# Attention with two gated layers: the stacking transfers in another order, and one turn on GpSimd alone

## The chip, the cores and the metric

The kernel runs on one core of one Trainium2 chip. The metric is the device time of one execution in microseconds (us). A core has the engines TensorE (PE in the profile, its weight loads PEld), VectorE (DVE), ScalarE (ACT), GpSimd (POOL) and SyncE (SP, which here issues every DMA transfer).

## The reference

Four batches, eight heads, 576 positions, 64 numbers per head. The reference rotates q and k by position, takes the softmax attention, and puts the result through two dense layers with gates and a normalisation. Cut to what matters here:

```
q_rot, k_rot = rotate(q), rotate(k)
scores = (1/8) * q_rot @ k_rot^T                       # per batch and head, 576 x 576
attn = exp(scores - rowmax) / (rowsum + 1e-9)
x = (attn @ v) as 2304 tokens x 512
x = (sigmoid(x @ w_gate) * (x @ w_val)) @ w_out         # d_ff 1536
h = x @ w_in; s = h * softmax(h); out = layernorm(s) * g_ln @ w_out2
```

## The kernel before

The work is in three stages. The attention stage goes over 16 **pairs** of heads, each pair in 9 tiles of query rows (four of 128 rows for each head, and in the middle one tile of the 64 left-over rows of both heads). The gate stage and the last stage follow.

fp32 operands are split into a high part (fp32r, made by ScalarE, the `CAST`s of L431) and a low part (the rest, made by VectorE, the `TENSOR_TENSOR`s of L434), so that a product is high x high + high x low + low x high. For the scores of head `h`, TensorE wants high and low parts of k or q on top of one another in the 128 partitions. The first tile of a pair (`st0`: blocks `flat[0]` to `flat[3]` = high k, high q, low k, low q, with head 0 in partitions 0 to 63 and head 1 in 64 to 127) is filled by the evacuations of three transpositions (`qk_bank`: `tq` on TensorE, L303 and L306). Then `stack` moves halves between partitions by DMA: the rows of head 1 go out of `st0` into the second tile `st1`, and when they have been read, the rows of head 0 are copied into the places they left. Those two last transfers (L318, L319 of the kernel before) overwrite what the first three read, so SyncE waits for these before it issues them. The first scores of a pair (L369, tile 0) read `st0` in full: the first product reads what L318 wrote, the second what L319 wrote. From there on TensorE goes on in order; a product that waits holds everything behind it.

Before the transpositions q and k are turned (`turn`: two products, L245, into `other` and in place, then a difference and a sum, L253, into `turned`). For pairs 2 to 15 GpSimd does that, while the pair before is computed. Pair 0 is turned at the start by VectorE and GpSimd together; pair 1 in the kernel before by GpSimd (head 0) and, after the first row maximum, by VectorE (head 1).

The order on each engine is written out by hand: an agenda of slots relative to the pair's first tile (`SLOTS`, L534 on), which the loop at L719 goes through tile by tile: row maximum (L376, VectorE), evacuations (ScalarE, then the exponentials, then VectorE), the next tile's scores on TensorE, then the rest of the slot, among it the DMA issues on SyncE. All instructions of an engine run in the order in which they were issued, and SyncE's too.

The sums of the exponentials (one column of `sum` for each tile) are inverted, transposed, written to a small DRAM buffer and spread over the partitions by DMA (`spread`, L416), by which GpSimd scales the attention's output (L426). GpSimd also makes the low part of v (L287), copies the left-over columns (L340) and adds the output's halves (L493).

Of the kernel before, what the change touches and what calls it, by code (L numbers as in the profile page):

```python
# [20 lines left out]
def kernel(  # L21
# [21 lines left out]
    nc = tc.nc  # L43
    B, H, S, D = q.shape
# [3 lines left out]
    P = 128  # L48
    MAIN, LEFT, HALF = 512, 64, 288
# [258 lines left out]
            src = ps[:, 0:P].rearrange("p (a t) -> p a t", a=2)  # L308
        return [(h_out, l_out, src)]

    def stack(i):
        s0, s1 = stacks[i, 0].bitcast(F32), stacks[i, 1].bitcast(F32)
        flat = s0.rearrange("p a b s -> p (a b) s")
        dma = nc.sync.dma_start
        dma(out=s1[D:P], in_=flat[D:P, 0:3])
        dma(out=s1[0:D, 0:2], in_=flat[D:P, 2:4])
        dma(out=s1[0:D, 2], in_=flat[D:P, 0])
        dma(out=flat[D:P, 0:2], in_=flat[0:D, 2:4])  # L318
        dma(out=flat[D:P, 2], in_=flat[0:D, 0])  # L319

    def stack_first(h, step):

# [23 lines left out]

    order = [(0, 0), (0, 1), (0, 2), (0, 3), None, (1, 0), (1, 1), (1, 2), (1, 3)]
    NTL = len(order)
    sum_at = [0, 1, 2, 3, 8, 4, 5, 6, 7]
    e_tiles = {}  # L350
    sums = {}
    wts = {}
# [26 lines left out]
    def exps(i, n, ps, nm):  # L379
        e = e_p.tile([P, S], F32, tag="e", name=f"e{i}_{n}")  # L380
        nc.scalar.activation(  # L381
            out=e.rearrange("p (j c) -> p j c", j=2),
            in_=ps[:, :, :HALF],
            func=AF.Exp,
            bias=nm,
            accum_out=sums[i][:, sum_at[n]:sum_at[n] + 1],
        )
        e_tiles[i, n] = e

# [21 lines left out]
    def spread(i):  # L411
        d = wts[i]
        w = wt_p.tile([P, S], F32, tag="wt", name=f"wt{i}")
        for c0, n, at in ((0, MAIN, 0), (MAIN, LEFT, 2 * MAIN)):
            for h in range(2):
                nc.sync.dma_start(  # L416
                    out=w[h * D:(h + 1) * D, c0:c0 + n],
                    in_=d[at + h * n:at + (h + 1) * n].unsqueeze(0).to_broadcast([D, n]),
                )
        wts[i] = w  # L420

    def scale_x(i):
# [107 lines left out]
    def at(g, kind, fn, *args):  # L530
        agenda.setdefault((g, kind), []).append((fn, args))
# [13 lines left out]
        scale=24,  # L545
        turn=(-16, -16, -15, -15),
        bank=(-11, -9, -8),
        stack=-6,
        split_v=-1,
        stack_left=0,  # L550
        load_qk=-23,
# [4 lines left out]
        sum_eng=0,  # L556
        uw=(1, 0, 0, 0),
        bank1=(1, 1, 1),
        stack1=3,
        first_b=(-1, -1, 2),  # L560
        turn1=(0, 0, 0, 0),
        split_v0=0,
        stack_left0=0,
    )
# [27 lines left out]
    for i in range(NPR):  # L592
        g = i * NTL
        own = SLOTS_FIRST if i == 0 else SLOTS_LAST if i == NPR - 1 else SLOTS
        for n in range(NTL):
            at(g + own["te"][n], FIRST, transpose_e, i, n)
        at(g + own["corner"], GROUP, transpose_corner, i)
        for h in range(2):
            at(g + own["left"][h], GROUP, transpose_left, i, h)
            for j in range(2):  # L600
                m0 = 0
                for slot, m1 in own["av"][2 * h + j]:
                    at(g + slot, ATTEND, attend, i, h, j, m0, m1)
                    m0 = m1
            at(g + own["join"][h], REST, join, i, h)
            at(g + own["add"][h], REST, add, i, h)
        for name, fn in (
            ("weigh", weigh), ("weigh_t", weigh_t), ("weigh_out", weigh_out), ("spread", spread), ("scale", scale_x)
        ):
            at(g + own[name], REST, fn, i)  # L610

        if i > 1:
            at(max(0, g + SLOTS["load_qk"]), REST, lambda i: [None for _ in load_qk(i)], i)
            at(max(0, g + SLOTS["load_v"]), REST, load_v, i)
            for m, slot in enumerate(SLOTS["turn"]):
                at(max(0, g + slot), REST, turn, i, m)
        if i > 0:
            for part, slot in enumerate(SLOTS["bank"] if i > 1 else [b - NTL for b in SLOTS["bank1"]]):
                at(g + slot, GROUP, qk_bank, i, part)
            at(g + (SLOTS["stack"] if i > 1 else SLOTS["stack1"] - NTL), REST, stack, i)  # L620
            at(g + SLOTS["split_v"], REST, split_v, i)
            at(g + SLOTS["stack_left"], REST, stack_left, i)
    cur, late, moved = [], [], []
# [62 lines left out]
    if True:  # L686

        spare_1 = et_p.tile([P, 16 * S], F32, tag="et", name="spare1")
        table = spare_1[:, 2 * NSL * D:2 * NSL * D + 2 * 5 * D // 2].rearrange("p (c i d) -> p c i d", c=2, i=5)
        first_loads = load_qk(0)  # L690
        next(first_loads)
        nc.sync.dma_start(out=table, in_=rope)
        for _ in first_loads:
            pass
        for h in range(2):
            nc.scalar.activation(out=rope_sb[:, :, h, 4:8], in_=table[:, :, 0:4], func=AF.Copy, scale=D ** -0.5)
        for _ in load_qk(1, spare_1[:, 0:2 * NSL * D].rearrange("p (h i d) -> p h i d", h=2, i=NSL)):
            pass
        nc.sync.dma_start(out=g_sb, in_=moe2_g_ln.rearrange("(k p) -> p k", p=P))
        load_v(0)  # L700
        load_v(1)
        turn_first(table)
        for h in range(2):
            nc.scalar.copy(out=rope_sb[:, :, h, 0:4], in_=table[:, :, 0:4])
            nc.scalar.copy(out=rope_sb[:, :, h, 8:9], in_=table[:, :, 4:5])
        first.extend(qk_bank(0, part)[0][2] for part in range(3))
        for m in range(3):
            stack_first(0, m)
            at(SLOTS["first_b"][m], REST, stack_first, 1, m)
        at(SLOTS["stack_left0"], REST, stack_left, 0)  # L710
        at(SLOTS["split_v0"], REST, split_v, 0)
        for m in range(4):
            turn(1, m, slice(0, 1))
            at(SLOTS["turn1"][m], REST, turn, 1, m, slice(1, 2), nc.vector)
        for fn, args in agenda.pop((-1, REST), []):
            fn(*args)

        sc = scores(0, 0)
        for g in range(NPR * NTL):  # L719
            i, n = divmod(g, NTL)  # L720
            if g == (NPR - 1) * NTL:
                prep_ctx.close()
                xs_pool["p"] = x_ctx.enter_context(tc.tile_pool(name="xs", bufs=XS, side="right", reuse_waits="tile"))
            if g == 1:
                et = et_p.tile([P, 2, 2, 4, S], F32R, tag="et", name="et")
            nm = row_max(i, n, sc)
            if SLOTS["exp_pos"] == 0:
                exps(i, n, sc, nm)
            evacuate_h(cur)
            if SLOTS["exp_pos"] == 1:  # L730
                exps(i, n, sc, nm)
            evacuate_h(late)
            if SLOTS["exp_pos"] == 2:
                exps(i, n, sc, nm)
            evacuate_u()
            if SLOTS["exp_pos"] == 3:
                exps(i, n, sc, nm)
            evacuate_l()
            if g + 1 < NPR * NTL:
                sc = scores(*divmod(g + 1, NTL))  # L740
            advance(g)
# [381 lines left out]
```

## Time and profile before

| what | value |
|---|---|
| time, median of 3 runs | 967.11 us (964.16 to 969.16) |
| the profiled execution's own time | 964.83 us |
| its span, first to last instruction | 963.1 us |
| busy over the span: PE, DVE, ACT, POOL | 96%, 67%, 52%, 46% |
| attention stage, roughly | 0 to 310 us |
| gate stage, roughly | 310 to 740 us |
| last stage | 740 to 963 us |

The page of the profile lists busy time by engine, forty slices of the span, the DMA queues, the chain of work that ended last (followed back from the last instruction to what released each one), groups of instructions by line with the idle time before them and who ended it, and the DMA issues with the time from issue to landing. In the slices of the attention stage, PE, DVE and ACT are each busy for eight or nine tenths and more, and POOL for seven to nine; in the other stages PE alone is full. Names such as `s`, `te`, `av`, `tq`, `st` are the kernel's tiles without their numbers, so `st` stands for `st0` and `st1` alike.

### The profile page before, as it was taken

The numbers are of one execution on the slowest core, as the hardware profiler recorded it, in microseconds if no ns is written. First come the engines' busy times: TensorE is split into PE (matmuls) and PEld (weight loads), VectorE is DVE, ScalarE is ACT, GpSimd is POOL, SyncE is SP. The second block draws the span as 40 slices with busy tenths as digits, with TensorE's granted clock in tenths as the row PEclk, the third lists the DMA queues.
The fourth block names the chain that finished last, engine by engine and source line by source line (L and its number), as shares of the span: only waits on it lengthen the run. The fifth ranks groups of instructions, "written<-read, shape, count | busy, mean of one in ns | idle before, by whom it ended". The sixth has DMA issues, their size and how long they took to land.

```text
span 963.1 us, 14429 instructions
## 1 busy us (share of the span) xinstructions
PE 923.1 (96%) x5128; PEld 801.5 (83%) x5128; DVE 647.7 (67%) x1073; ACT 501.7 (52%) x994; POOL 444.0 (46%) x356
## 2 busy tenths in 40 slices
PE   4999999899999899999999999999999989999998
PEld 3889889899898688898788898788898768888886
DVE  7999989999888955346345355545456787666661
ACT  4888989898987323133111123112123576666662
POOL 5668879889845533344324344324343531111110
PEclk9999999999999999999999999999999999999999
DMA  3666677676754310103101012100112334334332
GB/s 108 141 169 165 152 191 180 160 188 159 160 141 122 104 66 22 44 23 94 38 22 44 23 45 88 44 22 22 44 46 71 103 64 90 66 72 93 66 77 44
DMA packets 92311, 86.10 MB, mean 89 GB/s; under 512 B 52608, under 2 KB 77456, under 8 KB 92240
## 3 DMA queue, kind: packets, MB, share of 16 engines
q1 hardware_dynamic: 92240, 85.19, 35.7%
q8 instruction: 40, 0.66, 0.3%
q14 instruction: 31, 0.25, 0.1%
HBM read 46.83 MB, written 4.79 MB: 54 GB/s over the span
## 4 chain that ended last, share of the span: by engine, by line
PE 63%; DVE 14%; DMA 10%; POOL 4%; issue 4%; ACT 2%; SPq 2%; DVEq 0%; POOLq 0%; ACTq 0%
DMA st<-st 9%; PE gv L680 9%; PE gv L681 9%; PE gv L679 9%; PE y L790 4%; PE y L789 4%; PE y L788 4%; PE po L977 3%; PE po L976 3%; PE po L978 3%; PE ph L881 3%; PE ph L882 3%; PE ph L883 3%; DVE nm L376 3%; DVE et L434 2%
## 5 line engine op out<-in xcount | busy, mean ns | idle before, releaser
L774 POOL TENSOR_TENSOR gs<-g,gs 128x512 fp32r<-128x512 f32 (+1 forms) x59 | 74.1, 1257 | 261.2 <-DVE gs L773 203.9
L769 ACT ACTIVATE sg<-gv 128x512 f32<-128x512 f32 (+1 forms) x60 | 33.3, 555 | 288.2 <-PE gv L681 288.2
L679 PE MATMUL gv<-xs,w 128*128 128x512 f32 (+1 forms) x480 | 177.4, 370 | 2.1 <-ACT w L137 2.1
L681 PE MATMUL gv<-xs,w 128*128 128x512 f32 (+1 forms) x480 | 177.5, 370 | 1.2 <-POOL w L138 1.2
L680 PE MATMUL gv<-xs,w 128*128 128x512 f32 (+1 forms) x480 | 177.4, 370 | 1.0 <-DVE xs L514 1.0
L771 DVE TENSOR_TENSOR g<-gv,sg 128x512 f32<-128x512 f32 (+1 forms) x60 | 38.2, 636 | 174.5 <-ACT sg L769 164.9
L381 ACT ACTIVATE e<-s,nm 128x576 f32<-128x576 f32 x144 | 107.3, 745 | 16.9 <-DVE nm L376 16.4
L369 PE MATMUL s<-st 128*128 128x288 f32 x512 | 102.8, 319 | 13.8 <-DMA st<-st 7.0
L376 DVE TENSOR_REDUCE nm<-s 128x1 f32<-128x576 f32 x144 | 107.2, 745 | 5.5 <-PE s L369 4.0
L681 PEld LDWEIGHTS gv<-xs,w 128*128 128x128 f32 x480 | 90.9, 189 | 17.3 <-POOL w L138 2.1
L680 PEld LDWEIGHTS gv<-xs,w 128*128 128x128 f32 x480 | 90.5, 189 | 17.5 <-DVE xs L514 2.7
L679 PEld LDWEIGHTS gv<-xs,w 128*128 128x128 f32 x480 | 90.5, 188 | 17.4 <-ACT w L137 2.5
L434 DVE TENSOR_TENSOR et<-te,et 128x512 fp32r<-128x512 f32 x144 | 98.3, 684 | 9.7 <-ACT et L431 8.5
L481 PE MATMUL av<-et,vs 128*128 128x288 f32 x512 | 99.9, 316 | 0.3 <-DVE uw L632 0.3
L369 PEld LDWEIGHTS s<-st 128*128 128x128 f32 x512 | 75.3, 193 | 23.2 <-DMA st<-st 6.3
L790 PE MATMUL y<-gs,w 128*128 128x512 f32 (+1 forms) x240 | 88.3, 368 | 0.0
L789 PE MATMUL y<-gs,w 128*128 128x512 f32 (+1 forms) x240 | 88.2, 368 | 0.0
L788 PE MATMUL y<-gs,w 128*128 128x512 f32 (+1 forms) x240 | 88.2, 367 | 0.0
L440 PE MATMUL te<-ident,e 128*128 128x128 f32 x576 | 87.0, 274 | 0.7 <-DVE et L434 0.7
L431 ACT CAST et<-te 128x512 fp32r<-128x512 f32 x144 | 84.2, 586 | 5.3 <-PE te L440 5.2
L481 PEld LDWEIGHTS av<-et,vs 128*128 128x128 f32 x512 | 73.0, 189 | 1.6 <-DVE uw L632 1.0
L440 PEld LDWEIGHTS te<-ident,e 128*128 128x128 f32 x576 | 71.1, 141 | 1.1 <-DVE et L434 0.9
(128 smaller groups left out, 1958.1 us busy)
## 6 DMA issues: line engine op xcount, KB each, us to landing
wraw<-in_moe_w_out_dram SPq DMA_DIRECT2D x20, 512.0 KB, 4.6
st<-st SPq DMA_DIRECT2D x30, 288.0 KB, 3.1
st<-st SPq DMA_DIRECT2D x15, 432.0 KB, 4.0
wraw<-in_moe_w_gate_dram SPq DMA_DIRECT2D x12, 512.0 KB, 4.0
wraw<-in_moe_w_val_dram SPq DMA_DIRECT2D x12, 512.0 KB, 4.5
um<-uw SPq DMA_DIRECT2D x32, 144.0 KB, 2.4
st<-st SPq DMA_DIRECT2D x30, 144.0 KB, 4.9
rawv<-in_v_dram SPq DMA_DIRECT2D x16, 256.0 KB
```

Of the source, the lines that this page charges most:

```text
L369: nc.tensor.matmul(ps[:, j, :HALF], w, x, start=m == 0, stop=m == len(mm) - 1)
L376: nc.vector.tensor_reduce(out=nm, in_=ps[:, :, :HALF], axis=AX.XY, op=ALU.max, negate=True)
L381: nc.scalar.activation(out=e.rearrange("p (j c) -> p j c", j=2), in_=ps[:, :, :HALF], func=AF.Exp, bias=nm, accum_out=sums[i][:, sum_at[n] ...
L434: nc.vector.tensor_sub(out=l_out, in0=ps, in1=h_out.bitcast(F32))
L440: nc.tensor.transpose(ps[:, r * P:(r + 1) * P], e[:, r * P:(r + 1) * P], ident)
L481: nc.tensor.matmul(av[:, :HALF], *mm[m], start=m == 0, stop=m == len(mm) - 1)
L679: nc.tensor.matmul(ps[:, :n], wh, x[:, 0, :n], start=kk == 0, stop=False)
L680: nc.tensor.matmul(ps[:, :n], wh, x[:, 1, :n], start=False, stop=False)
L681: nc.tensor.matmul(ps[:, :n], wl, x[:, 0, :n], start=False, stop=kk == KD - 1)
L788: nc.tensor.matmul(ys[m][:, :n], wh, g[:, 0, :n], start=first, stop=False)
L789: nc.tensor.matmul(ys[m][:, :n], wl, g[:, 0, :n], start=False, stop=False)
L790: nc.tensor.matmul(ys[m][:, :n], wh, g[:, 1, :n], start=False, stop=last)
```

## The change

Three things change.

1. `stack` issues six transfers in place of five, in another order. The bytes are the same. The first two read only high parts, which ScalarE makes; the low parts, which VectorE makes, come with the third and the fourth. The transfer of 432 KB (three blocks) is divided into 288 KB and 144 KB, and the smaller one goes to the fourth place.
2. The columns of `sum` stand in the order of the tiles, so the left-over row comes in the middle, and `spread` needs three transfers in place of four.
3. GpSimd turns both heads of pair 1, with instructions twice as wide; VectorE's four instructions for head 1 go away.

```
     def stack(i, step):
         ...
-        dma(out=s1[D:P], in_=flat[D:P, 0:3])
-        dma(out=s1[0:D, 0:2], in_=flat[D:P, 2:4])
-        dma(out=s1[0:D, 2], in_=flat[D:P, 0])
-        dma(out=flat[D:P, 0:2], in_=flat[0:D, 2:4])
-        dma(out=flat[D:P, 2], in_=flat[0:D, 0])
+        if step == 0:
+            dma(out=s1[D:P, 0:2], in_=flat[D:P, 0:2])
+            dma(out=s1[0:D, 2], in_=flat[D:P, 0])
+            dma(out=s1[0:D, 0:2], in_=flat[D:P, 2:4])
+            dma(out=s1[D:P, 2], in_=flat[D:P, 2])
+        else:
+            dma(out=flat[D:P, 0:2], in_=flat[0:D, 2:4])
+            dma(out=flat[D:P, 2], in_=flat[0:D, 0])
...
-            accum_out=sums[i][:, sum_at[n]:sum_at[n] + 1],
+            accum_out=sums[i][:, n:n + 1],
...
-        for c0, n, at in ((0, MAIN, 0), (MAIN, LEFT, 2 * MAIN)):
-            for h in range(2):
-                nc.sync.dma_start(
-                    out=w[h * D:(h + 1) * D, c0:c0 + n],
-                    in_=d[at + h * n:at + (h + 1) * n].unsqueeze(0).to_broadcast([D, n]),
-                )
+        for h, c0, n, at in ((0, 0, S, 0), (1, 0, MAIN, S + LEFT), (1, MAIN, LEFT, S)):
+            nc.sync.dma_start(
+                out=w[h * D:(h + 1) * D, c0:c0 + n], in_=d[at:at + n].unsqueeze(0).to_broadcast([D, n])
+            )
...
-        stack=-6,
+        stack=(-6, -6),
...
-        stack1=3,
+        stack1=(3, 3),
...
         for m in range(4):
-            turn(1, m, slice(0, 1))
-            at(SLOTS["turn1"][m], REST, turn, 1, m, slice(1, 2), nc.vector)
+            turn(1, m)
```

Both steps of `stack` stand in the same slot, where the five transfers stood. The first place is SyncE's queue around the stacking of pair 3 (`st_3_679` or `st_3_676` is `st0`, `st_3_680` or `st_3_677` is `st1`; a name behind "waits" is what the instruction waits for, where DMAHW0 to DMAHW7 are eight counters of landed transfers). Before:

```order
L315 DMA st_3_680<-st_3_679 64x1728 [waits DMAHW3_49,DVE_49]
L316 DMA st_3_680<-st_3_679 64x1152 [waits DMAHW4_49]
L317 DMA st_3_680<-st_3_679 64x576 [waits DMAHW5_49]
L318 DMA st_3_679<-st_3_679 64x1152 [waits DMAHW6_49,DMAHW5_49,DMAHW3_49]
L319 DMA st_3_679<-st_3_679 64x576 [waits DMAHW7_49,DMAHW4_49]
```

And of the change:

```order
L317 DMA st_3_677<-st_3_676 64x1152 [waits Activation_49]
L318 DMA st_3_677<-st_3_676 64x576 [waits DMAHW5_49]
L319 DMA st_3_677<-st_3_676 64x1152 [waits DMAHW6_49,DVE_49]
L320 DMA st_3_677<-st_3_676 64x576 [waits DMAHW7_49]
L322 DMA st_3_676<-st_3_676 64x1152 [waits DMAHW5_49,DMAHW4_49,DMAHW0_49]
L323 DMA st_3_676<-st_3_676 64x576 [waits DMAHW7_49,DMAHW6_49,DMAHW1_49]
```

The first transfer now waits for ScalarE in place of VectorE, and the first of the two overwriting transfers now waits for the first and second reading transfer (counters 4 and 5; before: for the first and the third, counters 3 and 5), the second one for the third and fourth.

The second place is GpSimd's queue at the start, from the turn of pair 1 to that of pair 2, as a difference:

```order
-L245 TENSOR_TENSOR other_206<-spare_134,rope_sb 128x576 [waits DMAHW5_49,DMAHW0_49,DMAHW6_49,DVE_49,DMAHW7_49,Activation_49,Pool_49]
-L245 TENSOR_TENSOR spare_134<-spare_134,rope_sb 128x576 [waits Pool_49]
-L253 TENSOR_TENSOR turned_209<-spare_134,other_206 128x9x32 [waits PE_49,Pool_49]
-L253 TENSOR_TENSOR turned_209<-spare_134,other_206 128x9x32
...
+L245 TENSOR_TENSOR other_206<-spare_134,rope_sb 128x1152 [waits DMAHW5_49,DMAHW0_49,DMAHW6_49,DVE_49,DMAHW7_49,Activation_49,Pool_49]
+L245 TENSOR_TENSOR spare_134<-spare_134,rope_sb 128x1152 [waits Pool_49]
+L253 TENSOR_TENSOR turned_209<-spare_134,other_206 128x2x9x32 [waits PE_49,Pool_49]
+L253 TENSOR_TENSOR turned_209<-spare_134,other_206 128x2x9x32
```

The four instructions stay in their place and are twice as wide; on VectorE the four of head 1 (two of L245, two of L253) that stood between the first and the second row maximum are gone.

## Rows read from the trace of the kernel before

**Rows 1.** Busy time by stretch: stretch, length, then each engine's busy us (instructions), clock.
```profile
50.60:68.19 17.59, 16.81 (x131) 16.11 (x132) 16.17 (x28) 15.84 (x38) 13.19 (x10) 1.00 0.65 156
...
sum 246.74, PE 235.41 PEld 224.81 DVE 228.20 ACT 221.08 POOL 198.46; mean PE 16.81 PEld 16.06 DVE 16.30 ACT 15.79 POOL 14.18
...
330.00:740.00 410.00, 408.57 (x2004) 345.14 (x2003) 203.93 (x310) 95.30 (x175) 152.02 (x118) 1.00 0.14 46
```

**Rows 2.** Waits, 33 to 282 us: who for whom, total us, times, longest.
```profile
POOL vs L287 <- ACT vs L286: 32.0, 12, 7.6
...
PE s L369 <- DMA st<-st: 7.0, 16, 1.1
...
DVE uw L632 <- PE av L481: 5.4, 11, 0.6
```

**Rows 3.** SyncE's issues in order of time, stacking of pair 2: start, us, what.
```profile
40.40 0.54 SPq L315 DMA_DIRECT2D st<-st  x1
41.00 0.59 SPq L316 DMA_DIRECT2D st<-st  x1
41.64 1.67 SPq L317 DMA_DIRECT2D st<-st  x1
46.70 0.46 SPq L318 DMA_DIRECT2D st<-st  x1
47.26 0.54 SPq L319 DMA_DIRECT2D st<-st  x1
```

**Rows 4.** DMA issues of the page: times, KB each, median us from issue to landing.
```profile
st<-st SPq DMA_DIRECT2D x15, 432.0 KB, 4.0
um<-uw SPq DMA_DIRECT2D x32, 144.0 KB, 2.4
```

**Rows 5.** The chain of waits, 38 to 71 us: start, us, what.
```profile
41.64 5.01 DMA st<-st
...
47.26 3.30 DMA st<-st
...
50.60 0.67 PE s L369 x3
...
57.22 0.28 DVE st L434
```

**Rows 6.** The start in order of time, 10 to 29 us: start, us, engine, what.
```profile
10.18 1.40 POOL L245 TENSOR_TENSOR other<-spare,rope_sb 128x576 f32<-128x576 f32 x1 [1.51 <-DVE turned L253]
...
11.66 1.40 POOL L245 TENSOR_TENSOR spare<-spare,rope_sb 128x576 f32<-128x576 f32 x1
11.88 1.50 DVE L334 CAST st<-st 64x576 fp32r<-64x576 f32 x1
...
14.73 0.62 POOL L340 CAST qtl<-st 128x64 fp32r<-128x64 f32 x2
...
15.81 0.76 DVE L245 TENSOR_TENSOR other<-spare,rope_sb 128x576 f32<-128x576 f32 x1
...
17.34 1.57 POOL L287 TENSOR_TENSOR vs<-rawv,vs 128x640 fp32r<-128x640 f32 x1 [1.98 <-ACT vs L286]
17.39 2.20 DVE L253 TENSOR_TENSOR turned<-spare,other 128x288 f32<-128x288 f32 x2
...
19.73 2.64 POOL L245 TENSOR_TENSOR other<-raw,rope_sb 128x1152 f32<-128x1152 f32 x1 [0.82 <-DVE turned L253]
19.74 1.94 PE L303 MATMUL tq<-ident,turned 128*128 128x128 f32 x8 [1.72 <-DVE turned L253]
...
22.45 2.63 POOL L245 TENSOR_TENSOR raw<-raw,rope_sb 128x1152 f32<-128x1152 f32 x1
...
23.26 2.14 DVE L334 CAST st<-st 64x576 fp32r<-64x576 f32 x1
...
25.16 2.88 POOL L253 TENSOR_TENSOR turned<-raw,other 128x576 f32<-128x576 f32 x2
25.43 0.76 DVE L376 TENSOR_REDUCE nm<-s 128x1 f32<-128x576 f32 x1
```

More of the change, by code (lines that the diff above doesn't have):

```diff
@@ L309, in qk_bank, with stack @@
         return [(h_out, l_out, src)]
-    def stack(i):
+    def stack(i, step):
         s0, s1 = stacks[i, 0].bitcast(F32), stacks[i, 1].bitcast(F32)
@@ L348 @@
     NTL = len(order)
-    sum_at = [0, 1, 2, 3, 8, 4, 5, 6, 7]
     e_tiles = {}
@@ L558 @@
         bank1=(1, 1, 1),
-        stack1=3,
+        stack1=(3, 3),
         first_b=(-1, -1, 2),
-        turn1=(0, 0, 0, 0),
         split_v0=0,
@@ L619 @@
                 at(g + slot, GROUP, qk_bank, i, part)
-            at(g + (SLOTS["stack"] if i > 1 else SLOTS["stack1"] - NTL), REST, stack, i)
+            for step, slot in enumerate(SLOTS["stack"] if i > 1 else [s - NTL for s in SLOTS["stack1"]]):
+                at(g + slot, REST, stack, i, step)
             at(g + SLOTS["split_v"], REST, split_v, i)
```

## The prediction

> **What bounds the kernel now.** I read the busy time by stretch first. In the gate stage TensorE is busy for 408.57 of 410 us [rows 1], and the change doesn't touch it. The attention stage is another matter: over 14 pairs, 246.74 us, TensorE is busy for 235.41 and VectorE for 228.20, that is 16.81 and 16.30 us in a pair of 17.62 on average [rows 1]. So about 0.8 us of each pair is lost on the fullest engine, 11.3 us in all. Second, the waits in that stretch: 7.0 us of those 11.3 are TensorE's score products waiting for the stacking transfers, 16 times, at most 1.1 us [rows 2]. Third, SyncE's issues and the chain of waits, which show why these transfers are late. In pair 2 the first stacking transfer is issued at 40.40, the third lands at 41.64 + 5.01 = 46.65; only then is the first overwriting transfer issued (46.70), and the second one (47.26) lands 3.30 later, at 50.56. The score product starts at 50.60 [rows 3, 5]. From the first issue to the last landing that is 10.16 us. From the product at 50.60 the chain comes to the last evacuation of the next pair's transposes at 57.50 [rows 5], some 7 us, and there the next stacking starts. 10.2 + 7, and what lies between, is the pair's 17.59 us [rows 1]. The stage runs in a loop through the stacking, and TensorE's own 16.8 us are the next bound, close behind.
>
> **The stacking transfers.** Same bytes, one issue more, another order. The first three transfers of before, 432 + 288 + 144 = 864 KB, have all landed 6.25 us after the first issue (46.65 - 40.40), and the first 432 KB alone take 4.0 [rows 3, 4]. So data flows without a gap at 432 KB in 2.25 us, or 0.75 for 144 KB, and only the first transfer shows a fixed part, of about 1.75. Of the new order the first two are again 432 KB: landed at 4.0 to 4.1. The first overwriting transfer waits for these two alone and is issued at 4.1 in place of 6.3. Its 288 KB come behind the third and fourth transfer, which land at 6.25 as the same 864 KB did: 6.25 + 1.5 = 7.75. The second one is issued at 6.3. It then takes between 2.4 (a transfer of the same size alone, tile um [rows 4]) and 3.30 (the same transfer behind another's data [rows 5]), so it lands 8.7 to 9.6 after the first issue in place of 10.16. I take 8.9, since it is issued 2.2 us behind the other and that one is nearly through: 1.2 us earlier, the bounds 0.5 and 1.5. That covers the longest wait for one transfer, 1.1 us. So by the rows a transfer that queues behind others adds no fixed part: the second and third of before added 432 KB in 2.25 us [rows 3, 4]. The Trainium skill (DMA: Bandwidth & Descriptors, Anatomy of one DMA) says otherwise for a single one, some 2.0 us of fixed cost whatever its size, mostly for the receipt of the last byte, measured on transfers that GpSimd issues; if each of the six added its own, the sum would be a loss, by an estimate from the page 14 times 2.0 = 28 us. By the rows it is the gain worked out next, and the fourth rival is what is left of the doubt.
>
> The extra issue costs SyncE 0.5 to 0.6 us [rows 3] in a time in which it otherwise stands waiting for the landing; if that cover were gone, the loads behind it would be 0.6 later. The long issue of 1.67 [rows 3] comes with the transfer that goes past 720 KB; it will now be the fourth, which ends at about 3.4, still before 4.0. That the first two wait for ScalarE and not for VectorE gives up to 0.6 us more where SyncE is free, and nothing where it is busy issuing; I count nothing.
>
> What is it worth? At most the 7.0 us [rows 2]. At least nothing, if TensorE's lost time is only moved to a wait for VectorE or ScalarE, which are nearly as full. VectorE itself waits 5.4 us for TensorE in the same stretch [rows 2], behind such stalls, so they are not free. With the loop through the stacking open, a pair is held by TensorE's 16.8 and VectorE's 16.3 us; I take seven tenths: **4.9 us**.
>
> GpSimd, whose turns feed the next pair, is not in the way: at its low part of v it still waits for ScalarE, 32.0 us in 12 times [rows 2], and pairs shorter by 0.35 us take little of that.
>
> **The turn of pair 1.** VectorE loses four instructions between its first and second row maximum, from 15.81 to 19.59 [rows 6], 3.8 us in which nothing else of it runs; TensorE's transposes started behind them at 19.74. Now they wait for GpSimd. It starts at 10.18 as before, and its four instructions of full width take what they take for pair 2, from 19.73 to 28.04, 8.3 us [rows 6]: done at 18.5, with 0.25 us more if VectorE's copy gets between them. The transposes start 0.15 later, at 18.65 to 18.9: 0.8 to 1.1 us earlier. Next comes VectorE's copy at L334. It took 2.14 us at 23.26 and 1.50 at 11.88, and both times ended 0.32 after an instruction of GpSimd that was running (25.08 and 13.06) [rows 6]: it stands still while GpSimd's instruction lasts. The first copy is now held by an instruction that ends at 12.82, 0.2 us earlier than before. For the second: GpSimd is done with the turn at 18.5 to 18.75, its copies and low part of v (0.62 and 1.57 [rows 6]) take it to about 20.9, and its next instruction runs until about 23.6. The copy comes to its place at about 22.3 and ends 0.32 after that, at 23.9, where it ended at 25.40. So the row maximum that started at 25.43 is 1.5 us earlier. I take **1.3 us** for the start, between the 0.8 of the transposes and 1.7. Below that lies the third rival. GpSimd's turn of pair 2 ends 1 us later than before, 29.0 in place of 28.04; its cover is the time until those transposes come up in TensorE's order, some tiles on.
>
> **The sums' rows.** One column moved costs nothing. One issue fewer for each pair takes up to 0.6 us [rows 3] from SyncE while the scaling behind it, off the chain, waits for none of it: counted as nothing, 0 to 0.5 at the end of the last pair.
>
> **The sum.** 4.9 + 1.3 = 6.2 us of the profiled execution's 964.83 gives 958.6. That execution lies 2.3 under the median of the three runs, 967.11, from which the same sum gives 960.9. I forecast the median: 960.9 us. About 0.5%, 4.8 us, is what a measurement of this kernel can tell from no change.
>
> **The rivals.**
>
> First, the wait moves. The transfers land early, but TensorE then waits for VectorE's and ScalarE's results for nearly as long: both have only 1.3 to 1.8 us free in a pair [rows 1]. A fifth to a third of 7.0 stays, some 2 us, with the start 3.3: 963.8. For it speaks how equal the three engines are; against it the 5.4 us in which VectorE waits for TensorE [rows 2], which would shrink with the stalls.
>
> Second, the change doesn't do what it says: the overwriting transfers are not issued sooner. The queue still holds over 600 KB when SyncE comes to the first of them, and an issue in that state took 1.67 us in place of 0.5 [rows 3]. If this one stands until the queue has drained, it goes out near 6.3 as before and all of the gain in the loop is lost; only the start stays: 965.8. Against it: at 4.1 the first 432 KB have landed, and 432 KB of reads with 288 KB of writes make 720 KB, at which the second issue of before was still short (0.59).
>
> Third, a price at the start. GpSimd's instructions are twice as long, and VectorE's copy stands still behind whichever it meets. If the copy comes after 23.6 and not before, it meets the next one, which ends at about 26.3, and the row maximum is 1.2 us later than before and not 1.5 earlier; with the stacking's gain 963.4. It decides by a margin of about 1.3 us. The Trainium skill (SBUF — State Buffer, Who interferes with whom) has this as an exclusive port that the one who issues first keeps for its whole instruction; the two copies' lengths agree with that.
>
> Fourth, slower: the divided transfer pays for itself alone. If the fourth transfer's 144 KB take 2.4 us of their own behind the third [rows 4] and not 0.75, it lands at 7.9 in place of 6.25, and the second write, 3.3 behind that, at 11.25, 1.1 us later than before. This stands in the loop, so it comes back in each of 14 pairs: 15 us, less 1.3 from the start, 981. It decides at a landing of the fourth transfer 6.85 after the first issue. Against it: the second and third of before added 432 KB in 2.25 us with no such piece. The page's fixed part, named above, would do the same.
>
> **How the numbers follow.** The forecast 0.58, the first rival 0.18, the second 0.09, the third 0.08, the fourth 0.07. Within the forecast all of 7.0 and 1.7 would give 958.4; half of the wait and 0.8 give 962.8. A repeated median of three runs that lie 5 us apart moves by some 2 us. So the range goes from 956.5 to 966.5, which leaves out the fourth rival and the tails. Faster by over 0.5% means under 962.3: most of the forecast's cases, and few of the others', 0.60. Within 0.5%: 0.33. Slower: 0.07.
>
> **What would show it.** Right: TensorE's waits for the stacking transfers fall from 7.0 us to under 1; the second write lands about 8.9 us after the first issue; the pairs are 17.2 to 17.3 us long; the transposes of pair 1 start before 19, and the row maximum of 25.43 before 24.5. Wrong: the waits are gone and pairs are as long as before (first rival), the last landing is still at 10 us (second) or past it (fourth), or the copy at L334 lasts longer than 2.2 us (third).

## The result, and the profile after

The changed kernel takes 954.4 us (median of 4 runs, 952.74 to 954.9), the kernel before in the same comparison 968.13 (4 runs, 964.16 to 970.14). The ratio is 0.9867, 95% interval 0.9832 to 0.9903: about 13 us faster, where 6.2 were forecast. The direction is as predicted and so is the way the gain comes about; the size is about twice as large, and the time lies outside the range. The four runs of the kernel before lie high: in the comparisons of the experiments below (13 to 19 runs each) its median is 965.1 to 965.9, and against those the change gives about 11 us.

The profiled execution took 952.74 us. Of its page, the span, the busy time and the shares of the chain by engine:

```profile
span 951.0 us, 14440 instructions
...
PE 920.7 (97%) x5128; PEld 800.0 (84%) x5128; DVE 642.6 (68%) x1069; ACT 498.7 (52%) x994; POOL 446.7 (47%) x356
...
PE 77%; DVE 11%; POOL 6%; issue 3%; ACT 2%; DMA 1%; SPq 0%; POOLq 0%; DVEq 0%; ACTq 0%
```

The same shares in the kernel before:

```profile
PE 63%; DVE 14%; DMA 10%; POOL 4%; issue 4%; ACT 2%; SPq 2%; DVEq 0%; POOLq 0%; ACTq 0%
```

DMA has 1% of the chain now, and had 10%, so the chain no longer runs through the stacking transfers. Busy time by stretch, first of one pair, then of the 14 pairs from the first copy `rt<-tr` (VectorE makes one in each pair, so their distances are the pairs' lengths) to the last but one:

```profile
47.74:64.40 16.66, 16.66 (x132) 16.00 (x132) 15.61 (x28) 15.29 (x38) 13.20 (x10) 1.00 0.67 165
...
43.12:282.67 239.55, 235.37 (x1834) 224.21 (x1833) 228.77 (x389) 218.63 (x525) 193.64 (x149) 1.00 0.69 168
```

The same 14 pairs, between the same two copies, in the kernel before:

```profile
45.26:293.97 248.71, 236.22 (x1834) 225.07 (x1833) 228.35 (x388) 221.31 (x525) 194.68 (x149) 1.00 0.68 162
```

In the one pair TensorE is busy from end to end, 16.66 of 16.66 us. Over the 14 pairs the stage is 9.16 us shorter (248.71 - 239.55). Of these, 8.31 are TensorE's idle time (12.49 before, 4.18 now), and 0.85 are a shorter busy time for the same 1834 instructions, which I take for waiting that was recorded as work (no run shows it directly). The first copy comes 2.14 us earlier (45.26 and 43.12). So 9.16 + 2.14 = 11.3 of the 12.1 us between the spans; the rest is 0.3 in the last pair and some 0.5 after it.

Pairs one by one, worked out from the starts of these copies:

```
         pairs 1 to 14 of the stretch, then the last one                                  us
before   17.26 17.59 17.37 16.98 18.30 18.41 17.29 18.54 17.52 17.87 17.52 17.43 17.63 19.00 | 14.85
after    16.69 16.70 16.70 16.71 16.69 17.90 16.44 17.89 17.50 17.87 17.49 16.72 16.70 17.55 | 14.57
```

Seven of the fourteen are now 16.69 to 16.72 long, TensorE's own work. The six from the sixth to the eleventh are longer on average. In these the kernel also decodes the gate stage's first weights (six steps each, L122 to L138, on ScalarE, VectorE and GpSimd; one decoding begins every two pairs); of them the last three gained almost nothing. How the time falls on these six depends on the mark, since VectorE's copy comes later in every other one. The sixth and the seventh, where TensorE has 141 and 126 matmuls in place of 134:

```profile
126.61:144.51 17.90, 17.82 (x141) 16.98 (x140) 17.54 (x30) 15.43 (x38) 15.79 (x12) 1.00 0.75 181
144.51:160.95 16.44, 16.05 (x126) 15.05 (x124) 16.17 (x30) 15.86 (x39) 14.35 (x12) 1.00 0.77 195
```

Counted from one pair's second score product to the next one's, only three of the changed kernel's pairs are long, 17.45, 18.49 and 18.46; the others lie between 16.4 and 17.0. The fourteenth of the table (17.55) is a case of its own, in which the last stage of the pipeline of pairs runs out; TensorE's two waits for ScalarE in the next list, 0.7 us, both fall into it (at 269.56 and 275.53).

All of TensorE's own waits from 33 to 285 us, and GpSimd's longest:

```profile
POOL vs L287 <- ACT vs L286: 24.7, 12, 4.8
...
PE tq L303 <- DVE et L436: 2.6, 2, 1.3
PE s L372 <- ACT e L384: 0.7, 2, 0.4
PE tq L303 <- POOL x_sb L495: 0.2, 1, 0.2
```

The 7.0 us behind the stacking [rows 2] are gone to the last one, and little has taken their place: the waits for VectorE's `et`, 2.6 us, were 2.1 before, and they fall among the pairs with decoding (at 183.51 and 218.87; experiments below). SyncE's issues in the stacking of pair 2 and the first one of pair 3 show why:

```profile
38.27 0.54 SPq L317 DMA_DIRECT2D st<-st  x1
38.86 0.59 SPq L318 DMA_DIRECT2D st<-st  x1
39.55 0.81 SPq L319 DMA_DIRECT2D st<-st  x1
40.41 0.80 SPq L320 DMA_DIRECT2D st<-st  x1
42.38 0.46 SPq L322 DMA_DIRECT2D st<-st  x1
44.72 0.46 SPq L323 DMA_DIRECT2D st<-st  x1
...
54.13 0.60 SPq L317 DMA_DIRECT2D st<-st  x1
```

And the second write (L323), for which the view has the landing of one of the 15, in pair 10:

```profile
DMA to landing us min/median/max: 2.3/2.3/2.3
```

The first write goes out 4.11 us after the first issue (42.38 - 38.27; 6.30 before [rows 3]), the second 6.45 after it. With 2.3 us it lands at 47.02, that is 8.75 after the first issue in place of 10.16. The trace also has the semaphore counts of each transfer, 16 for one landing; the last count of this one stands at 8.76. The chain of waits at that place, which stood on the transfers before [rows 5], is TensorE alone:

```profile
47.12 0.50 PE tq L303 x4
47.61 0.73 PE s L372 x4
48.35 0.44 PE te L442 x4
```

The score product runs at 47.61 because TensorE comes to it then; its last operand landed 0.6 us before the first of these four matmuls. In pair 3 (first issue 54.13) the product that reads the second write starts 10.35 after the first issue, and by the counts that write lands 9.15 after it, so 1.2 us are spare; in pair 2 the same product starts 9.51 after the first issue, and 0.75 are spare.

At the start, in order of time:

```profile
10.21 2.62 POOL L245 TENSOR_TENSOR other<-spare,rope_sb 128x1152 f32<-128x1152 f32 x1 [1.51 <-DVE turned L253]
...
15.72 2.76 POOL L253 TENSOR_TENSOR turned<-spare,other 128x576 f32<-128x576 f32 x2
...
18.54 1.97 PE L303 MATMUL tq<-ident,turned 128*128 128x128 f32 x8 [0.74 <-POOL turned L253]
...
20.30 2.65 POOL L245 TENSOR_TENSOR other<-raw,rope_sb 128x1152 f32<-128x1152 f32 x1
22.09 1.19 DVE L338 CAST st<-st 64x576 fp32r<-64x576 f32 x1
...
23.30 0.76 DVE L379 TENSOR_REDUCE nm<-s 128x1 f32<-128x576 f32 x1
```

GpSimd's turn ends at 18.48, the transposes start at 18.54 in place of 19.74, and the row maximum that stood at 25.43 [rows 6] stands at 23.30.

### The profile page after: what moved, and what is told of

Read it like the earlier page. It is cut to its first block, busy times and chain, and to the rows that moved or that the text cites. A ratio compares the mean times of both kernels' runs of the same rounds, so it can differ in the third digit from the quotient of the medians.

```text
span 951.0 us, 14440 instructions
## 1 busy us (share of the span) xinstructions
PE 920.7 (97%) x5128; PEld 800.0 (84%) x5128; DVE 642.6 (68%) x1069; ACT 498.7 (52%) x994; POOL 446.7 (47%) x356
## 4 chain that ended last, share of the span: by engine, by line
PE 77%; DVE 11%; POOL 6%; issue 3%; ACT 2%; DMA 1%; SPq 0%; POOLq 0%; DVEq 0%; ACTq 0%
PE gv L682 9%; PE gv L683 9%; PE gv L681 9%; PE s L372 7%; PE av L483 6%; PE te L442 5%; PE y L789 4%; PE y L790 4%; PE y L791 4%; PE po L979 3%; PE po L978 3%; PE po L977 3%; PE ph L883 2%; PE ph L882 2%; PE ph L884 2%
## 5 line engine op out<-in xcount | busy, mean ns | idle before, releaser
L681 PEld LDWEIGHTS gv<-xs,w 128*128 128x128 f32 x480 | 90.8, 189 | 17.3 <-ACT w L137 2.2
L372 PE MATMUL s<-st 128*128 128x288 f32 x512 | 100.2, 318 | 5.2 <-ACT e L384 2.6
L683 PEld LDWEIGHTS gv<-xs,w 128*128 128x128 f32 x480 | 91.2, 190 | 16.4 <-POOL w L138 1.3
```

Source lines behind the costliest of these rows:

```text
L372: nc.tensor.matmul(ps[:, j, :HALF], w, x, start=m == 0, stop=m == len(mm) - 1)
L681: nc.tensor.matmul(ps[:, :n], wh, x[:, 0, :n], start=kk == 0, stop=False)
L683: nc.tensor.matmul(ps[:, :n], wl, x[:, 0, :n], start=False, stop=kk == KD - 1)
```

## The experiments

Two theories stood against each other. **The loop**: before, every pair without decoding ran from the stacking's first issue to its last landing and on to the next first issue, and when that way is shorter than TensorE's own work the pair falls to that work, whatever the listed waits add up to. **The listed waits**: as predicted, most of 7.0 us and no more, since VectorE and ScalarE are nearly as full. Each experiment was compared with the kernel before on the same chip; its median there lay between 965.1 and 965.9.

### The parts one by one

**p1_stack**: the kernel before with the new stacking alone.

```diff
-        dma(out=s1[D:P], in_=flat[D:P, 0:3])
-        dma(out=s1[0:D, 0:2], in_=flat[D:P, 2:4])
-        dma(out=s1[0:D, 2], in_=flat[D:P, 0])
+            dma(out=s1[D:P, 0:2], in_=flat[D:P, 0:2])
+            dma(out=s1[0:D, 2], in_=flat[D:P, 0])
+            dma(out=s1[0:D, 0:2], in_=flat[D:P, 2:4])
+            dma(out=s1[D:P, 2], in_=flat[D:P, 2])
...
```

The two writes stay, behind these.

> The kernel before with the new stacking alone. Theory A (the pair is a loop through the stacking; once its landing is early, TensorE runs without a gap at 16.7 us a pair): 9 to 10 us under before, TensorE's waits for the stacking at zero, pairs without decoding work 16.7 us long. Theory B (the stacking is worth what the stalls showed, at most 7.0, and the rest of the 13.7 comes from the start and the sums): 4 to 7 us under before, pairs of 17.1 to 17.3.

956.82 us, ratio 0.9898 (0.9869 to 0.9926): 8.3 us by the medians, 9.8 by the ratio. TensorE's wait for the stacking, from 33 to 285 us:

```profile
PE s L373 <- DMA st<-st: 0.2, 1, 0.2
```

Its 14 pairs are those of the changed kernel within 0.2 us, and together take 239.8 in place of 248.7:

```profile
45.08:284.85 239.77, 235.34 (x1834) 224.28 (x1833) 228.84 (x389) 218.79 (x525) 193.74 (x149) 1.00 0.69 168
```

The loop theory holds; 4 to 7 us does not.

**p2_turn**: the kernel before with GpSimd turning both heads of pair 1, and nothing else.

```diff
-            turn(1, m, slice(0, 1))
-            at(SLOTS["turn1"][m], REST, turn, 1, m, slice(1, 2), nc.vector)
+            turn(1, m)
```

> The kernel before with pair 1 turned by GpSimd alone. Theory A: the start ends 2.1 us earlier (the row maximum of tile 3 at 23.3 and not 25.4), and the loop through the stacking goes on at its own length from there, so 2 us under before and no more. Theory B: 3 us or more, since an earlier GpSimd or a freer VectorE helps later pairs too.

965.69 us, ratio 0.9991 (0.9970 to 1.0012): no difference that can be measured, though 1.5 us are inside the interval. In the profile the first copy `rt<-tr` comes 1.5 us earlier (43.73 and 45.26), and so does the last but one (292.47 and 293.97), yet the spans are only 0.2 us apart (962.9 and 963.1). The start gains as said, but it was not kept to the end of this execution: the last pair gives back 0.3 us and what follows it 1.1. There the granted clock was lower than in the profile of the kernel before, on average 0.84 against 0.92 over the 21.2 us after the last copy and 0.89 against 0.94 over 30 us of the last stage, because it stood longer at the lower of its two levels (1.2 GHz). So this profile can't tell what the start is worth alone, and the ten times show nothing of it. Meanwhile TensorE waits longer for the stacking than before:

```profile
PE s L369 <- DMA st<-st: 8.8, 19, 1.3
```

**p3_sums**: the kernel before with the new order of the sums and three spreading transfers in place of four.

```diff
-            accum_out=sums[i][:, sum_at[n]:sum_at[n] + 1],
+            accum_out=sums[i][:, n:n + 1],
...
-        for c0, n, at in ((0, MAIN, 0), (MAIN, LEFT, 2 * MAIN)):
...
+        for h, c0, n, at in ((0, 0, S, 0), (1, 0, MAIN, S + LEFT), (1, MAIN, LEFT, S)):
...
```

> The kernel before with the sums in tile order and three spreading transfers. Theory A: nothing that can be measured (within 1.5 us). Theory B: 1.5 to 3 us under before, because the spreading stands ahead of the stacking in SyncE's queue in some pairs and takes 0.6 us less.

963.8 us, ratio 0.9971 (0.9952 to 0.9989): some 2 us (1.3 by the medians, 2.8 by the ratio) for what the prediction counted as nothing. SyncE's queue shows a way. In the kernel before, the four spreading transfers stand right ahead of the next stacking in some of the pairs:

```profile
161.57 2.46 SPq L416 DMA_DIRECT2D wt<-d  x4
164.13 0.54 SPq L315 DMA_DIRECT2D st<-st  x1
```

With three of them, in p3_sums:

```profile
160.27 2.01 SPq L414 DMA_DIRECT2D wt<-d  x3
162.53 0.48 SPq L315 DMA_DIRECT2D st<-st  x1
```

The first stacking issue can be 0.45 us sooner there (2.46 - 2.01), and that is a place in the loop. TensorE's wait for the stacking is 4.6 us in 14 times, in place of 7.0 in 16.

**a1_noturn**: the change without the turn (new stacking and sums).

```diff
...
-            turn(1, m)
+            turn(1, m, slice(0, 1))
+            at(SLOTS["turn1"][m], REST, turn, 1, m, slice(1, 2), nc.vector)
```

> The changed kernel without the third part: new stacking and new sums' rows, pair 1 turned by GpSimd and VectorE as before. Theory A: pairs as in the changed kernel (16.7), the start 2 us later, so 1.5 to 2.5 us over the changed kernel; and within 1 us of the new stacking alone, since the sums' rows gave their 2.8 us only through the loop that is now open. Rival: the parts add up, so about 2.8 us under the new stacking alone.

956.71 us, ratio 0.9903 (0.9878 to 0.9929), the same as p1_stack's 956.82. So with the loop open the sums' issue is worth nothing that can be measured. From here to the whole change it is the turn alone: 956.71 to 954.4, 2.3 us by the medians of two comparisons, whose intervals overlap, and the first copy 2.0 us earlier (45.16 and 43.12). The parts do not add up: the sums count only while the loop is closed.

### Which property of the new stacking does it

**p4_five**: the five transfers of before, the second and third exchanged, nothing divided.

```diff
         dma(out=s1[D:P], in_=flat[D:P, 0:3])
-        dma(out=s1[0:D, 0:2], in_=flat[D:P, 2:4])
         dma(out=s1[0:D, 2], in_=flat[D:P, 0])
+        dma(out=s1[0:D, 0:2], in_=flat[D:P, 2:4])
```

> The kernel before with its five stacking transfers, of which only the second and third change places (432, 144, 288 KB). The first overwriting transfer then waits for 576 KB and not for 864. Theory A: what counts is when the two overwriting transfers may start, so nearly the whole gain of the new stacking, 7 to 10 us under before, landing about 8.8 us after the first issue. Theory B' (the division and the first wait for ScalarE carry it): under 3 us.

956.68 us, ratio 0.9900 (0.9875 to 0.9925): all of p1_stack's gain from two lines exchanged. SyncE in pair 2:

```profile
40.28 0.54 SPq L315 DMA_DIRECT2D st<-st  x1
...
45.21 0.46 SPq L318 DMA_DIRECT2D st<-st  x1
46.56 0.46 SPq L319 DMA_DIRECT2D st<-st  x1
```

The first write waits for 576 KB, and no longer for all 864, and goes out 4.93 us after the first issue in place of 6.30. Dividing the 432 KB and reading the high parts first are not needed for the gain.

**p5_order**: six transfers, but the 144 KB that the first write needs stand last, so that this write waits for all 864 KB again. What is left is the division, and that the first transfer waits for ScalarE and not for VectorE.

```diff
+            dma(out=s1[D:P, 0:2], in_=flat[D:P, 0:2])
+            dma(out=s1[0:D, 0:2], in_=flat[D:P, 2:4])
+            dma(out=s1[D:P, 2], in_=flat[D:P, 2])
+            dma(out=s1[0:D, 2], in_=flat[D:P, 0])
...
```

> The kernel before with six stacking transfers, divided as in the change and high parts first, but in such an order (288, 288, 144, 144 KB) that the first overwriting transfer waits for the first and the fourth, so for all 864 KB as before. Only the earlier first issue (it waits for ScalarE and not for VectorE) is left. Theory A (loop = 7.4 from the score product to the first issue + 10.15 to the last landing): the first part shortens by 0.5 to 0.9 us where SyncE is free, so pairs of 16.7 to 17.1 there and 17.4 where other issues stand ahead, 4 to 8 us under before. Rival (the order of the overwriting alone counts): within 1.5 us of before.

961.91 us, ratio 0.9962 (0.9938 to 0.9986): 4.0 us by the medians, 3.7 by the ratio.

```profile
40.30 0.54 SPq L317 DMA_DIRECT2D st<-st  x1
...
46.51 0.46 SPq L322 DMA_DIRECT2D st<-st  x1
47.08 0.54 SPq L323 DMA_DIRECT2D st<-st  x1
...
57.65 0.55 SPq L317 DMA_DIRECT2D st<-st  x1
```

TensorE's product at the end of this stacking:

```profile
50.47 0.65 PE L373 MATMUL s<-st 128*128 128x288 f32 x3 [0.36 <-DMA st<-st]
```

From the first issue to the writes it takes 6.21 and 6.78 us, nearly as before (6.30 and 6.86 [rows 3]). From the product to the next first issue it takes 7.18 (50.47 to 57.65), before 7.42 (50.60 to 58.02):

```profile
58.02 0.55 SPq L315 DMA_DIRECT2D st<-st  x1
```

In this pair it is the other end of the loop that is shorter, the first issue that no longer waits for VectorE. Over the 13 pairs from the second on, that end is 2.0 us shorter in all, and the way from the first issue to the product 2.6, most of it in the middle pairs; why there was not traced, so the earlier first issue is shown for a part of the 4.0 us only. Each way of shortening the loop pays, but the two together, 4.0 here and some 9 in p4_five, cannot give more than the way to TensorE's own work.

### How much slack is left

**d2_pad, d3_pad, d4_pad**: the changed kernel with one more transfer between reads and writes, 288, 432 and 576 KB into a DRAM buffer that nothing reads.

```diff
             dma(out=s1[D:P, 2], in_=flat[D:P, 2])
+            pad = dr_p.tile([D, 3, S], F32, tag="pad", name=f"pad{i}")
+            dma(out=pad, in_=flat[0:D, 0:3])
```

> The changed kernel with one more transfer of 288 KB in the stacking (two blocks to a DRAM buffer that nobody reads), between the reading and the overwriting transfers; what is computed stays. In the changed kernel the last landing is 8.7 us after the first issue and the score product comes up 10.2 after it: 1.5 us of slack. At 0.75 us for 144 KB the pad takes 1.5, so the landing goes to 10.2. Theory A (a hard loop: pair = the larger of TensorE's 16.7 and the loop): pairs stay at 16.7 to 16.8, time within 1.5 us of the changed kernel. Theory C (the three nearly full engines share every delay, half of it reaches the end): 17.0 to 17.4 in pairs without decoding work, 5 to 9 us slower.

> The same with 432 KB: the landing goes to 10.9, 0.7 past the slack. Theory A: each pair longer by what the landing exceeds 10.2, so about 17.4, and 6 to 10 us slower than the changed kernel. Theory C: by half of it, 17.0 to 17.1, 3 to 5 us.

> The same with 576 KB: the landing goes to 11.7, 1.5 past the slack. Theory A: pairs of 18.2, 15 to 20 us slower than the changed kernel and slower than the kernel before. Theory C: 17.4, 7 to 10 us.

```
          time us   ratio to before                over the change   first four pairs us
d2_pad    954.76    0.9873 (0.9832 to 0.9914)       0.4              16.70 17.10 16.87 16.70
d3_pad    961.17    0.9947 (0.9919 to 0.9975)       6.8              17.46 17.69 17.69 17.45
d4_pad    968.26    1.0028 (1.0007 to 1.0048)      13.9              18.18 18.19 19.99 18.31
```

In pair 2 of the changed kernel the product comes up 9.51 us after the first issue. With the pads the last landing of that pair (by the semaphore counts) is 9.57, 10.35 and 11.08 us after it, so 0.06, 0.84 and 1.57 late. The first four pairs are longer than 16.7 by 0 to 0.4, by 0.75 to 1.0, and by 1.5 to 1.6 but for one of 3.3. So there is a threshold, and behind it a price of about one for one. (The price of 0.75 us for 144 KB, worked out in the prediction, would make the delays 1.5, 2.25 and 3.0 us; measured against 8.76 they are 0.8, 1.6 and 2.3.) If TensorE shared delays with its neighbours, half of each would have shown from the first 288 KB on. In the one pair of 19.99 TensorE waited 1.67 us at its score product, and 1.0 us later the granted clock fell to the lower of its two levels (1.2 GHz) for 3.4 us; the same 134 matmuls, 16.8 us of busy time in its neighbours, are 18.32 there:

```profile
80.06:100.05 19.99, 18.32 (x134) 17.57 (x132) 16.12 (x29) 15.63 (x38) 16.36 (x13) 0.91 0.72 173
```

From pair 6 on, the landings of d4_pad are 10.7 to 11.3 us after the first issue, where those of pairs 2 to 5 are 11.1 to 12.2, and the whole stays under the 15 to 20 us that were expected; why they come earlier was not traced. In d3_pad the wait is back at its old place, in SyncE's queue of pair 2:

```profile
39.19 0.54 SPq L317 DMA_DIRECT2D st<-st  x1
...
45.65 0.63 SPq L325 DMA_DIRECT2D st<-st  x1
```

and on TensorE:

```profile
48.87 0.37 PE L374 MATMUL s<-st 128*128 128x288 f32 x1 [0.32 <-DMA st<-st]
49.57 0.67 PE L374 MATMUL s<-st 128*128 128x288 f32 x3 [0.34 <-DMA st<-st]
```

The product starts 10.38 us after the first issue, behind the landing. And d4_pad has about as much wait listed for the stacking as the kernel before (6.8 us in 12 times, against 7.0 in 16) and 0.3% more time: the whole gain is given back by a delay at this one place.

### What holds the pairs with decoding

Six steps of each decoding stand at slots 3, 5, 13, 15, 23 and 29, counted in tiles. Three runs change only that line of the changed kernel.

```diff
-        decode=(3, 5, 13, 15, 23, 29),
+        decode=(3, 5, 13, 15, 23, 34),
```

is b4_decode, in which only GpSimd's step is later, behind its turn; b1_decode has (3, 9, 18, 27, 32, 35), b3_decode (3, 5, 13, 24, 29, 34).

> The changed kernel with the decoding steps of the first gate weights at other tiles (9, 18, 27, 32, 35 in place of 5, 13, 15, 23, 29), so that VectorE's three steps fall into three pairs and not two into one, and GpSimd's step no longer stands between the two halves of a turn. In the changed kernel the six pairs with this work take 17.9, 16.4, 17.9, 17.5, 17.9 and 17.5 us, 4.9 us over six times 16.7. Theory A (TensorE is the bound wherever no other engine holds it): most of that comes back, 2 to 5 us under the changed kernel. Rival: VectorE and GpSimd are full in these pairs whatever the tile, and the time stays within 1.5 us.

> The changed kernel with the decoding steps at 5, 13, 24, 29 and 34: VectorE's third step a pair later, GpSimd's step behind the turn. VectorE then has at most 1.1 us more in a pair, about its slack beside TensorE's 16.7. Theory A: the six pairs with decoding take 16.8 to 17.3 in place of 17.5 on average, 1.5 to 4 us under the changed kernel. Rival (VectorE's instructions stand still behind GpSimd's whatever the tile): within 1.5 us.

> The changed kernel with GpSimd's decoding step alone moved from 29 to 34, behind the turn and not between its halves. If the late turn is what holds TensorE in these pairs (it waits 1.5 us for it in two of them), 1 to 3 us under the changed kernel; if VectorE is, nothing measurable.

```
             time us (4 runs)             ratio to before              the six pairs with decoding
change       954.4  (952.74 to 954.9)     0.9867 (0.9832 to 0.9903)    17.90 16.44 17.89 17.50 17.87 17.49
b1_decode    956.61 (956.15 to 956.71)    0.9891 (0.9860 to 0.9922)    17.10 17.38 17.74 18.42 17.74 18.43
b3_decode    951.94 (951.47 to 952.34)    0.9855 (0.9825 to 0.9884)    17.90 16.08 18.22 16.16 18.24 16.20
b4_decode    952.52 (951.31 to 954.25)    0.9863 (0.9836 to 0.9890)    17.92 16.42 17.86 16.43 17.89 16.43
```

b1_decode missed what was expected and is 2.2 us over the changed kernel; TensorE's longest wait in it, 2.9 us, is that of the transposes for VectorE's evacuations. b4_decode shows what two of the pairs lost. GpSimd and VectorE in the changed kernel, in order of time (two answers of the timeline):

```profile
177.06 1.73 POOL L138 TENSOR_TENSOR w<-val,w 128x512 fp32r<-128x512 f32 x1
178.75 2.80 POOL L253 TENSOR_TENSOR turned<-raw,other 128x576 f32<-128x576 f32 x2
...
180.36 1.74 DVE L126 SCALAR_TENSOR_TENSOR val<-wraw,val 128x512 int32<-128x512 int32 x1
```

and at the same step in b4_decode:

```profile
176.88 3.13 POOL L253 TENSOR_TENSOR turned<-raw,other 128x576 f32<-128x576 f32 x2
...
180.05 0.68 DVE L126 SCALAR_TENSOR_TENSOR val<-wraw,val 128x512 int32<-128x512 int32 x1
```

Where GpSimd's step stands ahead of the turn's second half (L253), the turn runs until 181.55, and VectorE's decoding step takes 1.74 us and ends at 182.10, 0.55 behind it. Where the turn is done at 180.01, the same step takes 0.68. Behind it VectorE's evacuation was late and TensorE waited, 2.6 us in two times; in b4_decode that wait is gone, and the two pairs of 17.5 are 16.43. b3_decode and b4_decode are the fastest medians of this study, some 2 us under the changed kernel. The intervals of the ratios overlap and the comparisons are different ones. In the profiles the 14 pairs of b4_decode take 2.2 us less (237.37 and 239.55), but the spans are only 0.7 apart (950.3 and 951.0), since the last pair and what follows it took longer in that execution. So the gain of the two pairs is shown, and one of the whole kernel is not. That three of the six still read 17.9 lies in the mark: from second score product to second score product the two long pairs fall from 18.49 and 18.46 to 17.40, and what is left are three pairs of 17.4. What holds these was not resolved; moving VectorE's decoding steps to another engine was not tried.

## Why the prediction was right and wrong

**The loop, right.** The way from first issue to last landing fell from 10.16 to 8.75 us (forecast 8.9), with the first write issued at 4.11 (forecast 4.1), by the continuous flow read from [rows 3, 4]. The extra issue is covered. That the kernel before ran in the loop shows in the semaphore counts: in 13 of its 15 stackings the second score product starts 0.04 us after the second write's landing. p4_five shows that earlier writes alone give the whole gain of the stacking. p5_order shows 4.0 us without them, partly from the first transfers' waiting for ScalarE, which the prediction counted as nothing; once the writes are early, this adds nothing that can be measured (p1_stack against p4_five).

**Its worth, wrong.** The failed step is "At most the 7.0 us [rows 2]", and then "I take seven tenths: 4.9 us", with pairs of "17.2 to 17.3". The stacking alone gave 8.3 to 9.8 us (p1_stack); in the changed kernel the 14 pairs are 9.16 us shorter in the profile, and the pairs without decoding are 16.7. Two things were misread. First, the listed waits were taken as a ceiling. Another 1.6 us of TensorE's waits in the kernel before stand under ScalarE's name, in two rows that the prediction left aside:

```profile
PE s L369 <- ACT st L431: 0.9, 1, 0.9
PE s L369 <- ACT et L431: 0.7, 2, 0.4
```

These three waits (at 67.45, 138.16 and 209.43) are those of a pair's first score product, and its stacking write had landed only 0.08 to 0.10 us before ScalarE's step ended: the same stop in the loop, put down to whichever came last (what made ScalarE's step late there was not traced). They too are gone with the new stacking alone, and so are 0.85 us of busy time, which I take for waiting recorded as work. The ceiling that the rows gave was the 11.3 us of lost time with which the prediction begins, and no row stood behind the seven tenths. Second, "TensorE's 16.8" has some waiting in it (busy for 16.77 to 16.81 us in each of the first five pairs before, 16.69 to 16.71 now); one pair with little stall, the fourth (16.98), already lay near the true 16.69. The working that the rows allowed: the loop was 10.15 us plus 7.4 from the score product to the next first issue (50.60 to 58.02 in the kernel before), 17.55; with the forecast's own 8.9 it comes to 16.3, under TensorE's 16.8, so each pair that nothing else holds falls to TensorE's own work. Measured it is 8.75 + 6.5 (47.61 to 54.13), 15.25.

**The first rival fell where nothing is decoded.** There the wait did not move to VectorE or ScalarE: both are near full, at 15.6 and 15.3 of 16.66 us, and still finish in time. Near full is not late. In the ninth to the eleventh pair, with decoding, it is what happened: they gained 0.05 us in all, and TensorE waits for VectorE there.

**The other rivals fell too.** The writes go out sooner (second). The copy at L338 came before GpSimd's next instruction and lasted 1.19 us, ending at 23.28, 0.33 behind the instruction that ended at 22.95 (third). The Trainium skill (SBUF — State Buffer, Who interferes with whom) has the port that the two engines share as a lock, which the one that issues first keeps for its whole instruction. The trace agrees here, and so does L126 above, which ends 0.55 us behind GpSimd's turn. The fourth transfer paid no fixed part of its own, or the second write could not have been issued 6.45 after the first issue (fourth); and p4_five, which divides nothing, is as fast as p1_stack. The Trainium skill (DMA: Bandwidth & Descriptors, Anatomy of one DMA) gives some 2.0 us of fixed cost for a transfer that GpSimd issues. The trace does not show as much for each transfer in SyncE's filled queue.

**The start, mechanism right, size small.** The transposes came at 18.54 (forecast 18.65 to 18.9), the row maximum 2.13 us earlier (forecast 1.5), since the copy ended at 23.28 and not 23.9: GpSimd's instruction in its way ended 0.65 us sooner than reckoned. The term was 1.3 and measured 2.1 to 2.3 with the loop open; with the old stacking (p2_turn) the first copy came 1.5 us earlier, and the times showed nothing.

**The sums' rows.** "Counted as nothing" is right in the whole change (a1_noturn equals p1_stack) and wrong alone (p3_sums): the same 0.5 us of issue is in the loop while the loop is closed and in slack when it is open.

## What to carry to other kernels

When an iteration is a loop through a chain of transfers, what opening it is worth is the iteration's length less the fullest engine's own work, taken from the iterations with least stall, and only for iterations that nothing else holds; the listed waits are not a ceiling, because one stall shows under several names. Inside the loop a delay on its way counts (behind the slack, the pads cost about one for one), and once it is open a delay counts for nothing until the slack is used, so parts measured alone do not add up. Where transfers overwrite what others read, put first the reads that the first write waits for: two exchanged lines gave 8 to 10 us here.

## What was not expected of the hardware

- The long issue of 1.67 us [rows 3] did not come back with the fourth transfer, where it was forecast. The third and the fourth take 0.81 and 0.80 us each; in p4_five, where the third transfer is the last of 864 KB, it is 1.69 again, and in p5_order the fourth takes 1.47. What makes an issue long was not settled.
- VectorE's step L126 took 1.74 us beside GpSimd's turn and 0.68 without it, and TensorE's busy time over the same 1834 matmuls was 236.22 us with stalls and 235.37 with fewer.
